# Half-height matmuls in pairs for the third input block of seven float32 first layers

## The chip, the cores and the metric

The kernel runs on one core of one Trainium2 chip. The metric is the device time of one execution in microseconds; lower is better. A time of the whole is the median of several runs. Times within the kernel come from one profiled execution, whose engines are named PE (TensorE's matmuls), PEld (its weight loads), DVE (VectorE), ACT (ScalarE), POOL (GpSimd) and SP (SyncE).

## The reference, cut to what matters

A gated recurrence with heads of width 40 gives 3072 rows of 320 numbers. Each row is then sent to one of 16 experts, whose network has a first layer of 320 x 1024, a Relu and a second layer of 1024 x 320.

```python
for g in range(G):
    ...
    for e in range(Eg):
        ...
        h = np.maximum(xg[mask_e] @ w1[g, e], 0.0)
        ye = h @ w2[g, e]
        combined = g_w[mask_g][mask_e] * e_w[mask_e]
        tok_idx = np.where(mask_g)[0][mask_e]
        out[tok_idx] = combined[:, None] * ye
```

All of it is float32: N = 3072, D = 320, F = 1024, G = Eg = 4.

## The kernel before, in words

The first third of the kernel is the recurrence in chunks (attention), in 24 units, with the choice of experts running beside it in an order written out by hand. Then `expert` runs for each of the 16 experts, largest first; `CAPS` holds how many rows each may take (the width W). From the third expert on, a scheduler orders the instructions.

An expert's rows are gathered from `x_d` in blocks of up to 128 (`load_x`), transposed on PE and copied to `xhl` (`turn_tasks`, lines 636 to 660), so that the 320 inputs stand on partitions in three blocks of 128, 128 and 64. The third block is stored twice over: `w1` is laid out on the host so that inputs 256 to 319 stand on partitions 0 to 63 and again on 64 to 127, and the rows in `x_d` repeat their last 64 columns in the same way (line 282).

Most experts run the first layer on values split into a high and a low part (float32r), and use the doubled third block for both parts. Experts 9 to 15, named by `FULL`, with W = 160, 144, 144, 144, 128, 128 and 96, run it in plain float32 instead (lines 679 to 688). There the upper half of the third block of `xhl` is set to zero by a GpSimd memset (line 652), and two ACT copies fill the rest (653, 654). For each pair of the eight output blocks, one bank of PSUM takes two halves of W columns, and each half sums three matmuls on all 128 partitions. Then `relu` (lines 670 to 677) reads the bank: ACT writes the Relu as the high part of `hh` (672), DVE subtracts to get the low part (675), in one or two instructions. After each pair one piece of the split of the next expert's `w2` is issued (`between`: an ACT cast at 611 and a DVE subtraction at 613). When the first layer has been issued, the next expert's transposes follow (`then`), and after them the second layer (lines 740 to 748), the scaling of `y` (752 to 756) and the scatter into the output (551).

PSUM has eight banks. `ps_1` holds two (`lg`, `av`) throughout. While attention runs, six more hold its scores, `Cp` and `avT`. `close_attention` gives those six to `ps_t` (one, for transposes, tile `tp`), `ps_h` (three, tile `psh`) and `ps_o` (two, tile `po`). The order in which the pools are opened decides which of the old banks each one gets.

Two lines of attention serve as comparison below: `scores` (line 182) multiplies float32 tiles of 40 rows that lie on partitions 0 to 39 and 64 to 103 in turn, into two banks; `values` (line 231) and `state` (line 204) use all rows and 40 or 41 columns; the filling matmuls `busy` (line 130) use the whole array in bfloat16.

Of the kernel before, what the change touches and what calls it, by code (L numbers as in the profile page):

```python
# [7 lines left out]
F32 = mybir.dt.float32  # L8
# [7 lines left out]
PSUM = bass.MemoryType.PSUM  # L16
DRAM = bass.MemoryType.DRAM

P = 128
# [6 lines left out]
F = 1024  # L26
# [27 lines left out]
FULL = (9, 10, 11, 12, 13, 14, 15)  # L54
# [7 lines left out]
def lstm_moe(ctx: ExitStack, tc: tile.TileContext, gates, qkT, nat, wcat, w1, w2, cst, seq, out):  # L62
    nc = tc.nc
    enter = ctx.enter_context
    mm = nc.tensor.matmul
# [32 lines left out]
    ps_1 = enter(tc.tile_pool(name="ps_1", bufs=1, space=PSUM))  # L98
# [24 lines left out]
    pools = {}  # L123
# [140 lines left out]
    def turned(tp, x, cols=(0, P, 2 * P)):  # L264
        for k, o in enumerate(cols):
            ins = nc.tensor.transpose(out=tp[:, k, :], in_=x[:, o:o + P], identity=ident)  # L266
        return ins
# [18 lines left out]
    chores, backs = [], []  # L286

    def bank_of(tag):
        return (pools["t"] if tag == "tp" else ps_1).tile([P, 512], F32, name=tag)

    def logits(u, o, bank):
        for k in range(3):
# [343 lines left out]
    def turn_tasks(key, W, xg, banks=None):  # L636
        t = {}

        def one(i, o, m):
            if i == 0:  # L640
                pool = pools["xhl"][len(xhls) % len(pools["xhl"])]
                sh, dt = ([P, 3, W], F32) if key[0] in FULL else ([P, 3, 2, W], F32R)
                t["x"] = xhls[key] = pool.tile(sh, dt, name="xhl", bufs=1)
            xhl, g = t["x"], xg[i]
            if banks:
                tp = banks[i][:, 0:3 * P].rearrange("p (k t) -> p k t", k=3)
            else:
                tp = bank_of(("tp", "lg", "av")[i])[:, 0:3 * P].rearrange("p (k t) -> p k t", k=3)
            turned(tp, g)
            if key[0] in FULL:  # L650
                if i == 0:
                    nc.gpsimd.memset(xhl[64:P, 2, :], 0.0)
                nc.scalar.copy(xhl[:, 0:2, o:o + m], tp[:, 0:2, 0:m])
                nc.scalar.copy(xhl[0:64, 2, o:o + m], tp[0:64, 2, 0:m])
                return
            xh = xhl[:, :, 0, o:o + m]
            nc.scalar.copy(xh, tp[:, :, 0:m])
            nc.vector.tensor_tensor(xhl[:, :, 1, o:o + m], tp[:, :, 0:m], xh.bitcast(F32), op=ALU.subtract)

        return [lambda i=i, o=o, m=m: one(i, o, m) for i, (o, m) in enumerate(blocks(W))]  # L660

    def expert(key, W, ws, xg, idx, between=(), then=None, last=None):
        xhl = xhls[key]
# [6 lines left out]
        def relu(f, per, src):  # L670
            hr = hh[:, f:f + per, 0:W]
            act = nc.scalar.activation(hr, src, AF.Relu)  # L672
            for dst, t in ((slice(W + mp, 2 * W), slice(0, nf)), (slice(W, W + mp), slice(nf, W))):
                if t.start < t.stop:
                    nc.vector.scalar_tensor_tensor(hh[:, f:f + per, dst], src[:, :, t], 0.0, hr.bitcast(F32)[:, :, t],  # L675
                                                   op0=ALU.max, op1=ALU.subtract)
            return act

        if key[0] in FULL:
            w1s = w1st[key[0]]  # L680
            for f in range(0, NF, 2):
                ps = pools["ps_h"].tile([P, 512], F32, name="psh")
                for g in range(2):
                    for k in range(3):
                        s = slice(k * F + (f + g) * P, k * F + (f + g + 1) * P)
                        ins = mm(ps[:, g * W:(g + 1) * W], w1s[:, s], xhl[:, k, :], start=(k == 0), stop=(k == 2))  # L686
                relu(f, 2, ps[:, 0:2 * W].rearrange("p (q w) -> p q w", q=2))
                do(between, 1)
        elif key in NARROW:
            xw, xh = [xhl[:, k].rearrange("p a w -> p (a w)") for k in range(3)], [xhl[:, k, 0, :] for k in range(2)]  # L690
            for f in range(0, NF, 2):
                hs = pools["hp"].tile([P, 2, W], F32, name="hs", bufs=2)
                for g in range(2):
                    ps = pools["ps_h"].tile([P, 512], F32, name="psh")
                    s0 = slice((f + g) * P, (f + g + 1) * P)
                    s1 = slice(F + (f + g) * P, F + (f + g + 1) * P)
                    mm(ps[:, 0:2 * W], w1h[:, s0], xw[0], start=True, stop=False)
                    mm(ps[:, 0:W], w1l[:, s0], xh[0], start=False, stop=False)
                    mm(ps[:, 0:W], w1l[:, s1], xh[1], start=False, stop=False)
                    mm(ps[:, 0:2 * W], w1h[:, s1], xw[1], start=False, stop=False)  # L700
                    ins = mm(ps[:, 0:2 * W], wsk[:, s0], xw[2], start=False, stop=True)
                    nc.scalar.copy(hs[:, g, :], ps[:, W:2 * W])
                    nc.vector.tensor_tensor(hs[:, g, :], hs[:, g, :], ps[:, 0:W], op=ALU.add)
                act = relu(f, 2, hs)
                if key[0] == 0:
                    do(between, 1)
        else:
            per = 2 if W <= 256 else 1
            for f in range(0, NF, per):
                ps = pools["ps_h"].tile([P, 512], F32, name="psh")  # L710
                for g in range(per):
                    s0 = slice((f + g) * P, (f + g + 1) * P)
                    s1 = slice(F + (f + g) * P, F + (f + g + 1) * P)
                    xh, xl = [xhl[:, k, 0, :] for k in range(3)], [xhl[:, k, 1, :] for k in range(3)]
                    todo = [(w1h, s0, xh[0]), (w1h, s0, xl[0]), (w1h, s1, xh[1]), (w1h, s1, xl[1]), (wsk, s0, xh[2]),
                            (wsk, s0, xl[2]), (w1l, s0, xh[0]), (w1l, s1, xh[1])]
                    for n, (w, s, x) in enumerate(todo):
                        ins = mm(ps[:, g * W:(g + 1) * W], w[:, s], x, start=(n == 0), stop=(n == len(todo) - 1))  # L718
                relu(f, per, ps[:, 0:per * W].rearrange("p (q w) -> p q w", q=per))
                if per == 2 or f % 2:  # L720
                    do(between, 1)
# [8 lines left out]
        for i, (o, m) in enumerate(blocks(W)):  # L730
            t = slice(o, o + m)
            tl = slice(W + mp + o, W + mp + o + m)
            po = pools["ps_o"].tile([P, DM], F32, name="po")
            for f in range(NF):
                s = slice(f * DM, (f + 1) * DM)
# [3 lines left out]
                if m > 64:  # L739
                    mm(po[0:m], hh[:, f, t], w2h[:, s], start=st0, stop=False)  # L740
                    mm(po[0:m], hh[:, f, t], w2l[:, s], start=False, stop=False)  # L741
                    ins = mm(po[0:m], hh[:, f, tl], w2h[:, s], start=False, stop=sp0)  # L742
# [202 lines left out]
    pools["ws"] = [wsa]  # L945
    pools["xhl"] = [mxp]

    def close_attention():
        att.close()
        pools["t"] = enter(tc.tile_pool(name="ps_t", bufs=1, space=PSUM, reuse_waits="tile"))  # L950
        pools["hp"] = enter(tc.tile_pool(name="hp", bufs=1, reuse_waits="tile"))
        pools["ws"].append(enter(tc.tile_pool(name="wsb", bufs=1, reuse_waits="tile")))
        pools["xhl"].append(pools["hp"])
        pools["ps_h"] = enter(tc.tile_pool(name="ps_h", bufs=3, space=PSUM, reuse_waits="tile"))
        pools["ps_o"] = enter(tc.tile_pool(name="ps_o", bufs=2, space=PSUM, reuse_waits="tile"))

    late_ix = {}

# [87 lines left out]
        expert((1, 0), CAPS[1], wsp_[1], xgs[1], ix_of(1), rest, turn_tasks((2, 0), CAPS[2], xgs[2]), done)  # L1046
    rt["manual"] = False
    for r in range(NEARLY + 1, NE):
        if r + 2 < NE:
            load_e(r + 2)  # L1050
            load_ix(r + 2)
            if r not in FULL:
                load_w1(r + 2)
            load_w2(r + 2)
            xgs[r + 2] = load_x(CAPS[r + 2], ix_of(r + 2))
        if r + 1 < NE:
            split = split_tasks(r + 1)
            if r + 1 not in FULL:
                do(split, 3)
            then = turn_tasks((r + 1, 0), CAPS[r + 1], xgs[r + 1])  # L1060
        else:
            then = []
        if r in FULL and r + 2 < NE:
            then.append(lambda r=r: load_w1(r + 2))
        expert((r, 0), CAPS[r], wsp_[r], xgs[r], ix_of(r), split, then)
# [7 lines left out]
    def plain(w1s, w2s, xT):  # L1073
        h = hp.tile([P, NF, P], F32, name="hh")
        for f in range(NF):
            ps = pools["ps_h"].tile([P, 512], F32, name="psh")
            for k in range(3):
                kk = min(P, DM - k * P)
                mm(ps[:, 0:P], w1s[0:kk, k * F + f * P:k * F + (f + 1) * P], xT[0:kk, k, :], start=(k == 0),
                   stop=(k == 2))  # L1080
            nc.vector.tensor_scalar(h[:, f, :], ps[:, 0:P], 0.0, None, op0=ALU.max)
        po = pools["ps_o"].tile([P, DM], F32, name="po")
        for f in range(NF):
            mm(po, h[:, f, :], w2s[:, f * DM:(f + 1) * DM], start=(f == 0), stop=(f == NF - 1))
        return po
# [202 lines left out]
```

## Time and profile before

| | us |
|---|---|
| median of 3 runs (370.94 to 371.11) | 370.95 |
| profiled execution | 368.52 |
| its span, first to last instruction | 366.9 |
| PE busy | 351.4 |
| DVE busy | 247.9 |
| ACT busy | 185.7 |
| POOL busy | 140.7 |

A group of instructions is read as: source line, engine, operation, output<-inputs, shape of the output and input (partitions x elements; for matmuls rows*columns of the stationary operand, then partitions x elements of the moving one), and xcount. Busy time counts overlapping instructions once. Matmuls are pipelined: the next one starts before the last one's end, so the pace is read from starts. The trace shows each float32 matmul as two, with a weight load before each.

### The profile page before, as it was taken

The page shows a single profiled execution, that of the slowest core. Times are in us where ns is not written, and L with a number is a line of the kernel's source. Part 1 is how long each engine was busy: PE and PEld are TensorE (multiplying, and loading weights), DVE is VectorE, ACT ScalarE, POOL GpSimd, SP SyncE. Part 2 cuts the span into 40 slices and gives each one's busy share as a digit, 9 for nine tenths or more (in the row PEclk, how much of TensorE's full clock was granted, in tenths as well). Part 3 has the DMA queues.
Part 4 walks back from the last instruction along what each step waited for, and adds up shares of the span by engine and source line. Part 5 has one row for each costly group of instructions (what it writes and reads, how often), then busy time and mean ns, then how long its engine had stood idle before and what let it go on. Part 6 is the DMA issues. An engine that isn't in the chain of part 4 may idle for free.

```text
span 366.9 us, 9390 instructions
## 1 busy us (share of the span) xinstructions
PE 351.4 (96%) x3572; PEld 318.5 (87%) x3572; DVE 247.9 (68%) x641; ACT 185.7 (51%) x447; POOL 140.7 (38%) x196
## 2 busy tenths in 40 slices
PE   7988999999997999999999999999999999999993
PEld 3766777777775999999999999999999999999992
DVE  6777977999898688577967566765646553365410
ACT  2534445365454363558557466755747454255520
POOL 2354355554664065732234445051223252224111
PEclk9999999999999899999999999999999999999999
DMA  6886787499694705990499765775552678667500
GB/s 191 268 267 248 221 263 274 138 324 301 169 319 127 329 3 195 321 346 31 155 413 397 260 237 208 261 260 171 205 172 66 238 290 326 244 211 289 191 19 17
DMA packets 26407, 82.23 MB, mean 224 GB/s; under 512 B 8528, under 2 KB 12131, under 8 KB 22514
## 3 DMA queue, kind: packets, MB, share of 16 engines
q1 hardware_dynamic: 17794, 60.32, 47.7%
q0 software_dynamic: 4848, 16.05, 12.4%
q10 hardware_dynamic: 3712, 5.18, 4.1%
q8 instruction: 30, 0.49, 0.5%
q14 instruction: 23, 0.19, 0.1%
HBM read 72.70 MB, written 9.10 MB: 223 GB/s over the span
## 4 chain that ended last, share of the span: by engine, by line
PE 62%; DMA 13%; issue 10%; DVE 8%; POOL 3%; ACT 1%; POOLq 1%; SPq 0%; DVEq 0%; ACTq 0%
PE psh L718 11%; PE psh L686 8%; DMA xg<-x_d,ix 6%; PE po L741 6%; PE po L742 6%; PE po L740 6%; PE sp L182 4%; DMA itab<-ent,slot 3%; PE avT L231 3%; PE po L746 2%; PE av L239 2%; DMA x_d<-x 2%; PE av L266 2%; PE po L745 2%; PE Cp L204 1%
## 5 line engine op out<-in xcount | busy, mean ns | idle before, releaser
L551 POOL DMA_INDIRECT out_dram<-y,ix x32 | 38.3, 1196 | 73.9 <-ACT y L752 58.5
L740 PE MATMUL po<-w2h,hh 128*128 128x320 f32 (+3 forms) x200 | 63.0, 315 | 0.0
L742 PE MATMUL po<-w2h,hh 128*128 128x320 f32 (+3 forms) x200 | 61.9, 309 | 0.0
L741 PE MATMUL po<-w2l,hh 128*128 128x320 f32 (+3 forms) x200 | 61.8, 309 | 0.0
L547 POOL DMA_INDIRECT xg<-x_d,ix x32 | 35.2, 1100 | 66.0 <-DMA ix<-itab 30.7
L613 DVE TENSOR_TENSOR w2l<-w2s,w2h 128x640 fp32r<-128x640 f32 x64 | 50.2, 815 | 10.9 <-ACT w2h L611 10.8
L675 DVE SCALAR_TENSOR_TENSOR hh<-psh,hh 128x240 fp32r<-128x240 f32 (+6 forms) x108 | 36.3, 365 | 22.4 <-ACT hh L672 19.7
L672 ACT ACTIVATE hh<-psh 128x288 fp32r<-128x288 f32 (+8 forms) x68 | 30.2, 444 | 34.0 <-PE psh L718 14.6
L611 ACT CAST w2h<-w2s 128x640 fp32r<-128x640 f32 x64 | 43.1, 722 | 0.0
L686 PE MATMUL psh<-xhl,w1s 128*128 128x144 f32 (+3 forms) x336 | 41.3, 283 | 0.0
L686 PEld LDWEIGHTS psh<-xhl,w1s 128*128 128x128 f32 x336 | 40.9, 191 | 0.0
L718 PE MATMUL psh<-xhl,w1h 128*128 128x256 f32 (+5 forms) x224 | 37.8, 291 | 0.4 <-DVE ewi L520 0.4
L740 PEld LDWEIGHTS po<-w2h,hh 128*128 128x128 f32 (+3 forms) x200 | 36.0, 180 | 0.0
L742 PEld LDWEIGHTS po<-w2h,hh 128*128 128x128 f32 (+3 forms) x200 | 35.9, 180 | 0.1
L741 PEld LDWEIGHTS po<-w2l,hh 128*128 128x128 f32 (+3 forms) x200 | 36.0, 180 | 0.0
L752 ACT ACTIVATE y<-po,ix 128x320 f32<-128x320 f32 (+3 forms) x24 | 12.7, 528 | 44.2 <-PE po L742 36.5
L187 DVE TENSOR_TENSOR pt<-sp,cs 128x512 f32<-128x512 f32 x48 | 30.6, 678 | 3.3 <-PE sp L182 3.3
L718 PEld LDWEIGHTS psh<-xhl,w1h 128*128 128x128 f32 x224 | 31.8, 193 | 0.9 <-PE psh L718 0.7
L452 POOL DMA_INDIRECT itab<-ent,slot x24 | 25.3, 1052 | 18.2 <-DVE ohs L375 10.4
L182 PE MATMUL sp<-qk 40*128 40x128 f32 x384 | 28.4, 285 | 0.2
L182 PEld LDWEIGHTS sp<-qk 40*128 40x128 f32 x384 | 23.6, 187 | 4.7 <-issue 3.3
L755 DVE TENSOR_TENSOR y<-y,po 32x320 f32<-32x320 f32 (+1 forms) x8 | 3.8, 475 | 33.9 <-ACT y L754 30.4
(215 smaller groups left out, 711.1 us busy)
## 6 DMA issues: line engine op xcount, KB each, us to landing
w1s<-in_w_dram SPq DMA_DIRECT2D x13, 1536.0 KB
w2s<-in_w_dram SPq DMA_DIRECT2D x13, 1280.0 KB
nt<-in_nat_dram SPq DMA_DIRECT2D x24, 480.0 KB
qk<-in_qkT_dram SPq DMA_DIRECT2D x48, 160.0 KB
x_d<-x ACTq DMA_DIRECT2D x12, 384.0 KB
w1s<-in_w_dram POOLq DMA_DIRECT2D x2, 1536.0 KB
w2s<-in_w_dram POOLq DMA_DIRECT2D x2, 1280.0 KB
w1s<-in_w_dram SPq DMA_DIRECT2D x4, 384.0 KB
```

Of the source, the lines that this page charges most:

```text
L182: mm(t["pm"][r][:, pr, :], qk[rs, 0, pr, :], qk[rs, 1, pr, :], start=True, stop=True)
L187: nc.vector.tensor_tensor(pt, t["pm"][r], bc(cs[:, C_UP:C_UP + P].unsqueeze(1), (P, 4, P)), op=ALU.mult)
L547: return nc.gpsimd.indirect_dma_start(out=o, out_offset=None, in_=src, in_offset=bass.IndirectOffsetOnAxis(ap=idx, axis=0))
L551: return nc.gpsimd.indirect_dma_start(out=out, out_offset=bass.IndirectOffsetOnAxis(ap=idx, axis=0), in_=y, in_offset=None, bounds_check=N ...
L611: nc.scalar.copy(a, src[:, s])
L613: lows.append(lambda: nc.vector.tensor_tensor(o[rows], src[rows, s], a[rows].bitcast(F32), op=ALU.subtract))
L675: nc.vector.scalar_tensor_tensor(hh[:, f:f + per, dst], src[:, :, t], 0.0, hr.bitcast(F32)[:, :, t], op0=ALU.max, op1=ALU.subtract)
L686: ins = mm(ps[:, g * W:(g + 1) * W], w1s[:, s], xhl[:, k, :], start=(k == 0), stop=(k == 2))
L718: ins = mm(ps[:, g * W:(g + 1) * W], w[:, s], x, start=(n == 0), stop=(n == len(todo) - 1))
L740: mm(po[0:m], hh[:, f, t], w2h[:, s], start=st0, stop=False)
L741: mm(po[0:m], hh[:, f, t], w2l[:, s], start=False, stop=False)
L742: ins = mm(po[0:m], hh[:, f, tl], w2h[:, s], start=False, stop=sp0)
```

## The change

In the first layers of experts 9 to 15 the third input block is multiplied on 64 partitions: for the even output block on partitions 0 to 63, for the odd one on 64 to 127. The two output blocks of a pair get a PSUM bank each, so a buffer is two banks. The order within a pair becomes: blocks 0 and 1 of the even one, blocks 0 and 1 of the odd one, then the two half-height matmuls one after the other. The upper half of the third block is now used, so the memset goes, and one copy moves all three parts. The pools `ps_t` and `ps_h` are closed before expert 9, and a new pool of two buffers of two banks takes their four; from there on transposes use the banks of `lg` and `av`. So that this is possible `ps_o` is opened first. `plain`, which no row reaches with these inputs, takes its bank from the new pool.

```diff
     def bank_of(tag):
-        return (pools["t"] if tag == "tp" else ps_1).tile([P, 512], F32, name=tag)
+        if tag == "tp" and "t" in pools:
+            return pools["t"].tile([P, 512], F32, name=tag)
+        return ps_1.tile([P, 512], F32, name="lg" if tag == "tp" else tag)
...
-                tp = bank_of(("tp", "lg", "av")[i])[:, 0:3 * P].rearrange("p (k t) -> p k t", k=3)
+                tp = bank_of(("tp", "lg", "av")[i if "t" in pools else i + 1])[:, 0:3 * P].rearrange("p (k t) -> p k t", k=3)
             turned(tp, g)
             if key[0] in FULL:
-                if i == 0:
-                    nc.gpsimd.memset(xhl[64:P, 2, :], 0.0)
-                nc.scalar.copy(xhl[:, 0:2, o:o + m], tp[:, 0:2, 0:m])
-                nc.scalar.copy(xhl[0:64, 2, o:o + m], tp[0:64, 2, 0:m])
+                nc.scalar.copy(xhl[:, :, o:o + m], tp[:, :, 0:m])
                 return
...
             for f in range(0, NF, 2):
-                ps = pools["ps_h"].tile([P, 512], F32, name="psh")
-                for g in range(2):
-                    for k in range(3):
-                        s = slice(k * F + (f + g) * P, k * F + (f + g + 1) * P)
-                        ins = mm(ps[:, g * W:(g + 1) * W], w1s[:, s], xhl[:, k, :], start=(k == 0), stop=(k == 2))
-                relu(f, 2, ps[:, 0:2 * W].rearrange("p (q w) -> p q w", q=2))
+                ps = pools["ps_h"].tile([P, 2, 512], F32, name="psf")
+                for k, g in ((0, 0), (1, 0), (0, 1), (1, 1), (2, 0), (2, 1)):
+                    s = slice(k * F + (f + g) * P, k * F + (f + g + 1) * P)
+                    rs = slice(0, P) if k < 2 else slice(64 * g, 64 * g + 64)
+                    ins = mm(ps[:, g, 0:W], w1s[rs, s], xhl[rs, k, :], start=(k == 0), stop=(k == 2))
+                relu(f, 2, ps[:, :, 0:W])
                 do(between, 1)
...
+    narrow = ExitStack()
+
     def close_attention():
         att.close()
-        pools["t"] = enter(tc.tile_pool(name="ps_t", bufs=1, space=PSUM, reuse_waits="tile"))
+        pools["ps_o"] = enter(tc.tile_pool(name="ps_o", bufs=2, space=PSUM, reuse_waits="tile"))
+        pools["t"] = narrow.enter_context(tc.tile_pool(name="ps_t", bufs=1, space=PSUM, reuse_waits="tile"))
         pools["hp"] = enter(tc.tile_pool(name="hp", bufs=1, reuse_waits="tile"))
         pools["ws"].append(enter(tc.tile_pool(name="wsb", bufs=1, reuse_waits="tile")))
         pools["xhl"].append(pools["hp"])
-        pools["ps_h"] = enter(tc.tile_pool(name="ps_h", bufs=3, space=PSUM, reuse_waits="tile"))
-        pools["ps_o"] = enter(tc.tile_pool(name="ps_o", bufs=2, space=PSUM, reuse_waits="tile"))
+        pools["ps_h"] = narrow.enter_context(tc.tile_pool(name="ps_h", bufs=3, space=PSUM, reuse_waits="tile"))
...
     for r in range(NEARLY + 1, NE):
+        if r == FULL[0]:
+            narrow.close()
+            del pools["t"]
+            pools["ps_h"] = enter(tc.tile_pool(name="ps_f", bufs=2, space=PSUM, reuse_waits="tile"))
```

## Rows read from the trace of the kernel before

**Rows 1.** The page, part 1: busy us (share of the span) x instructions.

```profile
PE 351.4 (96%) x3572; PEld 318.5 (87%) x3572; DVE 247.9 (68%) x641; ACT 185.7 (51%) x447; POOL 140.7 (38%) x196
```

**Rows 2.** Table by stage: stretch, length, PE, PEld, DVE, ACT, POOL, clock, DMA, GB/s.

```profile
0.00:118.00 118.00, 111.19 (x1773) 83.88 (x1773) 98.60 (x302) 54.00 (x174) 58.90 (x113) 1.00 0.75 238
...
283.25:356.90 73.65, 73.65 (x574) 72.09 (x573) 33.79 (x77) 33.58 (x80) 19.21 (x21) 1.00 0.62 227
```

**Rows 3.** Chain of waits, from 280 us: start, length, what.

```profile
283.41 6.52 PE psh L686 x48
...
361.41 0.85 POOL out_dram L551
```

**Rows 4.** Table by stretch of line 686 alone: length, PE, PEld, clock, DMA, GB/s.

```profile
283.25:289.77 6.52, 6.52 (x48) 6.44 (x48) 1.00 0.61 225
308.67:314.55 5.88, 5.88 (x48) 5.82 (x48) 1.00 0.62 231
333.09:338.44 5.35, 5.35 (x48) 5.32 (x48) 1.00 0.75 273
351.50:356.80 5.30, 5.30 (x48) 5.30 (x48) 1.00 0.08 30
```

**Rows 5.** Timeline of PE: start, length, line, operation; expert 9's and 14's first layers.

```profile
283.11 0.31 PE L746 MATMUL po<-w2h,hh 128*128 128x320 f32 x1
283.25 6.68 PE L686 MATMUL psh<-xhl,w1s 128*128 128x160 f32 x48
...
342.29 5.52 PE L686 MATMUL psh<-xhl,w1s 128*128 128x128 f32 x48
```

**Rows 6.** Timeline of one unit's scores and the two matmuls before them.

```profile
47.62 0.28 PE L231 MATMUL avT<-pt,vz 128*41 128x128 f32 x2
47.83 0.97 PEld L182 LDWEIGHTS sp<-qk 40*128 40x128 f32 x16 [0.19 <-issue]
47.83 1.16 PE L182 MATMUL sp<-qk 40*128 40x128 f32 x16
```

**Rows 7.** Instructions of line 182: duration in ns, shortest/median/longest, first and last start.

```profile
L182 PE MATMUL sp<-qk x384: 272/272/373, 7.0 to 113.0; 40*128 40x128 f32 x192
```

**Rows 8.** Timeline: from scores to matmuls on all rows, twice.

```profile
7.89 0.28 PE L182 MATMUL sp<-qk 40*128 40x128 f32 x2
8.10 0.10 PEld L130 LDWEIGHTS <-ones_b 128*128 128x128 bf16 x1
...
85.16 0.61 PE L182 MATMUL sp<-qk 40*128 40x128 f32 x8
...
85.70 0.14 PEld L266 LDWEIGHTS av<-cs,x 128*128 128x128 f32 x1
85.71 0.33 PE L266 MATMUL av<-cs,x 128*128 128x128 f32 x1
```

**Rows 9.** Timeline: from matmuls of 41 columns to a transpose.

```profile
45.75 0.20 PE L204 MATMUL Cp<-vz,nt 128*40 128x41 f32 x1
45.88 0.42 PEld L239 LDWEIGHTS av<-cs,avs 128*128 128x128 f32 x4
```

**Rows 10.** Timeline of DVE: low parts, second pair of expert 11, first of expert 14.

```profile
312.95 0.51 DVE L675 SCALAR_TENSOR_TENSOR hh<-psh,hh 128x224 fp32r<-128x224 f32 x2
...
345.14 0.42 DVE L675 SCALAR_TENSOR_TENSOR hh<-psh,hh 128x256 fp32r<-128x256 f32 x1
```

**Rows 11.** Instructions of line 652: duration in ns, shortest/median/longest, first and last start.

```profile
L652 POOL MEMSET xhl<- x7: 172/212/253, 263.1 to 338.7; 64x144 f32 x3, 64x128 f32 x2, 64x160 f32 x1, 64x96 f32 x1
```

**Rows 12.** Groups by line and shape, ACT, 283.25 to 357: busy us, mean ns, idle.

```profile
L654 ACT COPY xhl<-tp 64x112 f32<-64x112 f32 x3 | 0.7, 245 | 0.0
```

**Rows 13.** Timeline where attention closes.

```profile
120.25 1.09 DVE L658 TENSOR_TENSOR xhl<-Cp,xhl 128x384 fp32r<-128x384 f32 x2 [1.66 <-ACT xhl L657]
120.88 0.85 PE L266 MATMUL tp<-cs,x 128*128 128x128 f32 x3
121.38 1.20 PE L718 MATMUL psh<-xhl,w1h 128*128 128x256 f32 x4
```

More of the change, by code (lines that the diff above doesn't have):

```diff
@@ L1075, in plain @@
         for f in range(NF):
-            ps = pools["ps_h"].tile([P, 512], F32, name="psh")
+            ps = pools["ps_h"].tile([P, 2, 512], F32, name="psf")[:, 0]
             for k in range(3):
```

## The prediction, made before the change was run

> **What bounds the kernel now.** First the page: TensorE is busy 96% of the span [rows 1]. That share is a mean, so next the table by stage [rows 2]: from 283.25 to 356.90, the stage of experts 9 to 15 that the change rewrites, PE is busy for 73.65 of 73.65 us at granted clock 1.00, its 2.4 GHz level. DVE and ACT are busy less than half of it, and the DMA share is 0.62. Nothing ends a wait there, because PE does not wait. The chain of waits says the same: each first layer (L686) stands in it as one unbroken piece, that of expert 9 as 6.52 us, and the chain ends with the last scatter [rows 3]. So a microsecond more or less of PE in this stage is one more or less at the end. All the L686 time, by its four widths, is 6.52 + 3 x 5.88 + 2 x 5.35 + 5.30 = 40.2 us [rows 4].
>
> **How PE spends it.** Each expert has 8 output blocks x 3 input blocks = 24 matmuls in the source and 48 in the trace [rows 4]: a float32 matmul runs as two, each with a weight load of its own. Start to start they take p = 6.52/48 = 0.136 us at 160 columns, 0.1225 at 144, 0.1115 at 128 and 0.1105 at 96. The loads lie under the matmul before. A group's border costs nothing here: from L746 to L686 it is 0.14 us [rows 5].
>
> **Part 1: the third input block on row halves.** Per pair of output blocks the old order has 6 source matmuls, 12 starts at p. The new has 8 on all rows, then the third block's two source matmuls (4 starts) with 64 rows each, on different halves and into different banks. Do two such run beside each other? The score matmuls (L182) are the same form: float32, 128 weight columns, row halves taken in turn, two banks. Sixteen of them take 1.16 us from first start to last end, with single ones of 0.272 [rows 6, 7]: (1.16 - 0.27)/8 = 0.11 per pair, and two start within 0.01 us (the last two take 0.28 together, [rows 8]). So four starts become two. Saved: 2p per pair of blocks, four pairs per expert: 4 x 2 x (0.136 + 3 x 0.1225 + 2 x 0.1115 + 0.1105) = **6.7 us**, a sixth of 40.2.
>
> Next, what a change from all rows to half rows and back costs, since there is one in each direction per pair of blocks: 4 x 2 x 7 = 56. The attention stage has such changes. The last two L231 start at 47.62, and the first weight load of L182 starts at 47.83: 0.20 later, where inside a group it comes at once. Then that first matmul lasts 0.37 instead of 0.27 (272 ns median, 373 longest), because its load no longer lies under anything: 0.10 more [rows 6, 7]. Back from half rows to all rows: L182 ends at 85.77, so its last started at 85.50, and the load of L266 starts at 85.70: again 0.20 [rows 8]. Is that a wait for data? L182 to L130 at 8.10 needs nothing of the scores, and shows 7.89 to 8.10, 0.21 with the pair's own 0.01 [rows 8]. Where the last matmul is 41 columns wide the gap is 0.13 (45.75 to 45.88, [rows 9]); so it is 0.093 after the last stream's end, at 0.84 ns a column. It is a drain, and it comes with the change of shape of the array's use, not with the group: the border of [rows 5] has none.
>
> The Trainium skill, TensorEngine Tiling (Array Packing), Key Properties, says that changing the tiling mode, unlike changing the tile, drains TensorE. The trace agrees, with 0.20 us at 128 columns. TensorE: Matmul & The Clock Gate of the Trainium skill, step-by-step part, puts the drain at some 128 cycles, which is 0.053 us at 2.4 GHz (an estimate from that page) against 0.093 here; by it the sum below would be 56 x 0.04 = 2.2 us lower, and the rows decide.
>
> One change thus costs c = drain + 0.10 - p. At 128 columns: 0.20 + 0.10 - 0.11 = 0.19. At 144 the drain is 0.213 and p 0.1225: 0.19. At 160: 0.227 and 0.136: 0.19. At 96: 0.173 and 0.11: 0.16. The pair's offset adds 0.007. Net for a pair of blocks, 2c + 0.007 - 2p: +0.166 at 128, +0.148 at 144, +0.121 at 160, +0.113 at 96. Four pairs, seven experts: 4 x (0.121 + 3 x 0.148 + 2 x 0.166 + 0.113) = **+4.0 us**. The last change back of experts 9 to 14 meets the transposes, whose load shows 0.33 instead of 0.27, so 0.05 and not 0.10 [rows 8]: -0.3. Part 1: **+3.7**.
>
> **Part 2: banks.** Two buffers of two banks replace three of one, so a pair of blocks waits for the Relu and the subtraction of the pair before last, no longer of the third last. Queued behind that wait is all of PE. In expert 14 (PE from 342.29 [rows 5], 12 x 0.1115 = 1.34 per pair) DVE reads the first pair until 345.14 + 0.42 = 345.56 [rows 10]. The third pair started at 344.97, 0.59 too early for two buffers. With the longer pairs of part 1 (1.50) it starts at 345.30, 0.26 short. In a 144-wide expert (PE from 308.67) the second pair is read until 312.95 + 0.51 = 313.46 [rows 10] and the fourth would start at 308.67 + 3 x 1.618 = 313.52, just free. DVE and ACT are late because the w2 split stands ahead of them, and that queue empties the sooner the slower PE goes. Bounds: 0, and 0.59 in each of six experts, 3.5. I take **+0.3**, near the expert-14 row alone.
>
> **Part 3: no clearing, one copy.** Seven GpSimd memsets of 0.17 to 0.25 us go; PE waits for nothing in this stage [rows 2], so not for them, and behind them on that queue only scatters wait, which need a later `y` anyway [rows 11]. The two copies per gathered block become one over three parts; on ACT that saves some 0.2 us each for eleven blocks [rows 12], after the first layer, with 3.8 us or more before its result is read (expert 13's L686 ends at 338.44, expert 14's starts at 342.29, [rows 4, 5]). 0. If that cover went, 0.2 per expert. The transposes now take the `lg` and `av` banks, which nothing else uses then: 0.
>
> **Part 4: pools in another order.** When attention closes, the `tp` and `psh` tiles take banks that other tiles held, the `Cp` pair among them. `Cp` is read by DVE from 120.25 to 121.34; the transposes into `tp` start at 120.88 and the first `psh` matmul at 121.38 [rows 13]. The first reading is over before 120.9, the second before 121.38. Bounds 0 to 0.5 (`tp` behind both readings); I take 0.
>
> **The sum.** 3.7 + 0.3 = +4.0 us. The profiled execution took 368.52 us (span 366.9) and would take 372.5. The median of the runs shown, 370.95, lies 2.4 above it; added to that: **375.0 us**, 1.1% slower.
>
> **Rivals.** (a) *Two buffers bite.* The wait of part 2 in most experts at its upper bound: up to 378.2. For it: 0.59 at expert 14 [rows 10]. Against: PE itself becomes slower. 8%. (b) *The halves run one after the other*, or overlap by half, since each source matmul is two: 3.4 to 6.7 of the saving lost, 378.3 to 381.7. Against: [rows 7], eight pairs in eight slots. 3%. (c) *Faster: the next weights load during the drain.* A change then costs 0.09, not 0.19: 56 x 0.10 = 5.6 less, 369.4. It decides at 6.7/56 = 0.12 us per change: below it the change wins. For it: inside a group the load does run ahead. Against: in every change of shape shown the load starts behind the drain, with nothing to wait for in [rows 8]. 6%. (d) *Changes of shape cost nothing in a dense stream*: -6.7, 364.3. The same rows speak against it. 3%. The Trainium skill's same tiling page, Theoretical Speedup, names up to 2x for a small dimension of 64 or less, which is this case's result if nothing is paid around the pair. (e) *The drain is shorter than in attention*, some 0.04 each: 372.8, still slower. 4%. (f) The array stays in one shape and the halves run as before: pairs cost what they cost, within 0.2% of 370.95. 2%.
>
> **Chances and range.** The forecast itself has 74%. A measurement of this kernel tells about 0.2% (0.74 us) from no change. Slower: 74 + 8 + 3 + 4 = 89%; same 2% and a little from (c)'s upper end, 3%; faster 8%. The forecast's own spread is 373.9 to 376.5 (part 2 from 0 to 1, part 4, 0.01 us per change). For 8 in 10 it reaches a little into (e) and (a): 373.4 to 377.3.
>
> **What would show it.** After, an L686-like group at 144 columns takes 5.88 + 4 x 0.148 = 6.5 us instead of 5.88, at 128 some 6.0; the 64-row matmuls come in twos 0.01 us apart; 0.20 us of PEld idle stands before each first 64-row load and 0.2 before each return; the other stages are unchanged; the granted clock stays at 1.00, as it does in the first 118 us with all their changes of shape [rows 2]. Wrong: 64-row loads that start while full-row matmuls still stream (c, d), twos 0.11 apart (b), or PE waiting for DVE in the third or fourth pair by more than 0.3 (a).

## The result, and the profile after

The changed kernel takes 374.6 us (median of 4 runs) beside 370.94 for the kernel before: a ratio of 1.013, 95% interval 1.009 to 1.017. Slower, as forecast, and 0.4 us from the 375.0 on record. In a later set of runs, beside the second half of the experiments below, the medians were 376.85 and 370.11, the ratio 1.016, interval 1.008 to 1.024. Medians here and below are over all runs, while ratios, intervals and spreads leave out slow runs, which lie over 1.5% above the fastest of their kernel (two of the six behind 376.85; the other four have a median of 375.44).

The profiled execution took 373.16 us, span 371.5, against 368.52 and 366.9. Page, part 1, of the changed kernel (busy us, share of the span, instructions), to set beside [rows 1]:

```profile
PE 357.1 (96%) x3572; PEld 315.7 (85%) x3572; DVE 249.2 (67%) x641; ACT 185.6 (50%) x436; POOL 138.7 (37%) x189
```

The share of PE is the same and says nothing; its time is 5.7 us longer with the same number of instructions, while PEld's is shorter. Even the 5.7 is not the price of the change: 1.9 of it lie in the first 118 us (113.08 here, 111.19 in [rows 2]), where nothing was changed. The table by stage, with the columns of [rows 2], shows the stage that was rewritten:

```profile
0.00:118.00 118.00, 113.08 (x1772) 84.85 (x1772) 98.56 (x297) 54.06 (x174) 58.53 (x111) 0.99 0.77 236
283.71:364.90 81.19, 81.18 (x597) 71.70 (x595) 34.32 (x78) 33.75 (x72) 19.25 (x16) 1.00 0.56 206
```

(The second stretch also takes in the last second layer, which the one in [rows 2] does not.) PE is still taken for all of it, at granted clock 1.00, and PEld now stands still for 9.5 us of it. A time that hardly depends on what came earlier in the run is the length of this stage, from the first L686 (L685 after) to the start of the last matmul of the second layer. Timeline of PE, last matmul, of the kernel before and then of the changed one:

```profile
360.20 0.31 PE L742 MATMUL po<-w2h,hh 128*96 128x320 f32 x1
```

```profile
364.59 0.30 PE L741 MATMUL po<-w2h,hh 128*96 128x320 f32 x1
```

Before: 360.20 - 283.25 = 76.95 us ([rows 5] has the start). After: 364.59 - 283.71 = 80.88 us, and 80.88 again in the second profile of the changed kernel (285.35 to 366.23). The change costs **3.93 us** there. The rest of the difference of the two spans, 0.7 us, lies outside: 0.46 before the stage begins and 0.2 behind its last matmul.

Inside a pair of blocks, in expert 10 (144 columns), the timeline shows how the 3.93 comes about. PE, taken in short windows, then PEld. Rows of short windows overlap: the first holds the last matmul on all rows and the two half-height ones behind it; in the others x2 is one pair:

```profile
298.06 0.61 PE L685 MATMUL psf<-xhl,w1s 128*128 128x144 f32 x3
298.27 0.39 PE L685 MATMUL psf<-xhl,w1s 64*128 64x144 f32 x2
298.50 0.29 PE L685 MATMUL psf<-xhl,w1s 64*128 64x144 f32 x2
298.72 0.39 PE L685 MATMUL psf<-xhl,w1s 128*128 128x144 f32 x1
```

```profile
298.27 0.19 PEld L685 LDWEIGHTS psf<-xhl,w1s 64*128 64x128 f32 x2
298.38 0.19 PEld L685 LDWEIGHTS psf<-xhl,w1s 64*128 64x128 f32 x2
298.72 0.19 PEld L685 LDWEIGHTS psf<-xhl,w1s 128*128 128x128 f32 x1
```

The last matmul on all rows starts at 298.06 and the first load for half rows at 298.27: 0.21 later, where the working had 0.213 for this width. The next load follows at 298.38, so the first one held its matmul up by 0.1; that matmul lasts 0.39 and the second 0.29. Both halves of a pair start within 0.01 us (two take 0.39 and 0.29 together). From the second pair at 298.50 to the next load on all rows it is 0.22, the drain again with the pair's own offset. The second and the third pair of blocks of this expert take 1.62 us from first start to first start, where 12 x 0.1225 = 1.47 stood (the first pair takes 1.52, since its first load still lies under the matmul before).

One thing in the PE timeline of this expert was not foreseen:

```profile
297.20 4.83 PE L685 MATMUL psf<-xhl,w1s 128*128 128x144 f32 x36
301.96 0.40 PE L739 MATMUL po<-w2h,hh 128*112 128x320 f32 x1
302.36 1.59 PE L685 MATMUL psf<-xhl,w1s 128*128 128x144 f32 x12
```

Between the third and the fourth pair of blocks the scheduler has put the first matmuls of the second layer, which were ready, into the place where it reckoned with a wait for a buffer. No such wait is in the trace. In the table of waits of this stage (who, for whom: us in total, times, longest; short gaps are left out) the row of the first layer's loads names no reader of a bank, only gaps in which nothing is waited for:

```profile
PEld psf L685 <- issue: 1.0, 6, 0.2
```

### The profile page after: what moved, and what is told of

The parts are those of the page before. It is cut to its first block, busy times and chain, and to the rows that moved or that the text cites. A ratio compares the mean times of both kernels' runs of the same rounds, so it can differ in the third digit from the quotient of the medians.

```text
span 371.5 us, 9357 instructions
## 1 busy us (share of the span) xinstructions
PE 357.1 (96%) x3572; PEld 315.7 (85%) x3572; DVE 249.2 (67%) x641; ACT 185.6 (50%) x436; POOL 138.7 (37%) x189
## 4 chain that ended last, share of the span: by engine, by line
PE 69%; issue 12%; DVE 7%; DMA 5%; POOL 4%; ACT 1%; POOLq 1%; SPq 0%; DVEq 0%
PE psh L717 14%; PE po L739 7%; PE psf L685 7%; PE po L740 7%; PE po L741 7%; PE sp L182 3%; PE avT L231 3%; PE po L745 2%; PE av L266 2%; PE av L239 2%; PE po L744 2%; DMA itab<-ent,slot 2%; PE busy L130 2%; PE avT L222 2%; DMA ix<-itab 2%
## 5 line engine op out<-in xcount | busy, mean ns | idle before, releaser
L553 POOL DMA_INDIRECT out_dram<-y,ix x32 | 37.1, 1161 | 90.4 <-ACT y L751 74.8
L685 PE MATMUL psf<-xhl,w1s 128*128 128x144 f32 (+3 forms) x336 | 44.1, 303 | 0.0
L685 PEld LDWEIGHTS psf<-xhl,w1s 128*128 128x128 f32 x336 | 37.3, 188 | 5.9 <-issue 1.0
L674 DVE SCALAR_TENSOR_TENSOR hh<-psh,hh 128x240 fp32r<-128x240 f32 (+4 forms) x64 | 23.0, 390 | 9.8 <-ACT hh L671 9.7
L671 ACT ACTIVATE hh<-psh 128x512 fp32r<-128x512 f32 (+5 forms) x40 | 19.1, 479 | 17.3 <-PE psh L717 14.7
L231 PE MATMUL avT<-pt,vz 128*41 128x128 f32 x384 | 26.9, 281 | 0.9 <-DVE pt L187 0.7
```

The lines of the kernel that those rows point to most:

```text
L231: mm(placed(pr, r), t["vz"][:, head(pr, r), :], t["pm"][r][:, pr, :], start=(c == 0 and pr < 2), stop=True, skip_group_check=True)
L553: return nc.gpsimd.indirect_dma_start(out=out, out_offset=bass.IndirectOffsetOnAxis(ap=idx, axis=0), in_=y, in_offset=None, bounds_check=N ...
L685: ins = mm(ps[:, g, 0:W], w1s[rs, s], xhl[rs, k, :], start=(k == 0), stop=(k == 2))
```

## The experiments

All kernels below are timed against the kernel before on the same chip; its median was 371.64 beside the first four and 370.11 beside the others, where the table has the 370.94 of the first runs. For each, the stage is measured as above, in one profile, and lengths are taken before rounding. Some expectations name 73.5 us for this stage before (and 75.4, 77.5 or 69.3 after): they count it to about the end of the last first layer, some 3.4 us earlier, so their differences compare with those here and their lengths do not. Whole times of one kernel spread by several us from run to run (366.87 to 372.34 for the kernel before in the second set), and in the profiles the stage begins anywhere between 283.25 and 288.30, so the stage is what is read first.

| kernel | first and last start of the stage | stage, us | against before | median, us | ratio to before (95%) |
|---|---|---|---|---|---|
| before | 283.25, 360.20 | 76.95 | | 370.94 | |
| changed | 283.71, 364.59 | 80.88 | +3.93 | 374.6 | 1.013 (1.009 to 1.017) |
| all rows, two buffers | 287.33, 366.22 | 78.88 | +1.93 | 373.27 | 1.007 (1.003 to 1.011) |
| both on the same half | 284.44, 371.75 | 87.30 | +10.35 | 381.6 | 1.029 (1.024 to 1.035) |
| halves of two pairs together | 288.30, 367.52 | 79.22 | +2.27 | 376.65 | 1.015 (1.010 to 1.020) |
| all on half rows | 283.37, 367.58 | 84.20 | +7.25 | 378.61 | 1.024 (1.018 to 1.030) |
| all halves first | 284.64, 357.47 | 72.83 | -4.12 | 366.16 | 0.991 (0.987 to 0.996) |
| all rows, four buffers | 284.59, 361.54 | 76.95 | 0.00 | 369.72 | 1.001 (0.997 to 1.005) |
| halves apart | 284.94, 382.95 | 98.00 | +21.05 | 390.2 | 1.057 (1.048 to 1.066) |

The theory: each change between all rows and half rows costs PE some 0.19 us, 56 of them, against 6.7 us saved by the pairs. The rivals: the two buffers, halves that don't run beside each other, and the pools.

### All rows, two buffers

```diff
-                    rs = slice(0, P) if k < 2 else slice(64 * g, 64 * g + 64)
+                    rs = slice(0, P)
```

with the memset and the two copies of the kernel before.

> The changed kernel with the third input block back on all 128 rows (upper half cleared again by the memset, two copies), but the new pools, the two banks per buffer and the new order of matmuls kept. Theory (each change between all rows and half rows costs 0.19 us, 56 of them, against 6.7 us saved): both go, so 370.95 + 0 to 0.5, some 371.2 us, the first layer of a 144-wide expert back at 5.9 us. Rival (two buffers instead of three make PE wait): the loss stays, 374 to 375 us, with PE idle before the third and fourth pair.

Neither came out as stated; the rival was right in kind, but the loss is half of what it named. The stage takes 78.88 us, 1.93 over before, although no shape changes. PE's timeline of expert 10, and the largest entry of PE's loads in the table of waits:

```profile
300.59 4.76 PE L688 MATMUL psf<-xhl,w1s 128*128 128x144 f32 x36
305.10 0.40 PE L742 MATMUL po<-w2h,hh 128*112 128x320 f32 x1
305.55 1.71 PE L688 MATMUL psf<-xhl,w1s 128*128 128x144 f32 x12
```

```profile
PEld psf L688 <- DVE hh L677: 0.6, 2, 0.5
```

The row's 4.76 is 0.2 longer than 35 x 0.1225 and the 0.29 of the last matmul. In each of experts 9 to 14 some 0.3 us goes, to a wait for DVE's reading of the pair before last and to the second-layer matmuls that stand in the gap; most of the single waits are too short for the table. Where they stand can be seen in PE's timeline of the first two pairs and of the start of the third:

```profile
300.59 3.10 PE L688 MATMUL psf<-xhl,w1s 128*128 128x144 f32 x24
303.65 0.48 PE L688 MATMUL psf<-xhl,w1s 128*128 128x144 f32 x2
```

The first two pairs keep the old pace (23 x 0.1225 and the last matmul make 3.10). The third, which takes the first buffer again, could start at 300.59 + 24 x 0.1225 = 303.53; it starts 0.12 late, and its second matmul comes 0.20 behind the first, since a load that had to wait is not hidden. So two buffers do cost something, by themselves, with the faster pairs. The experiment with four buffers, below, takes this up.

### Both halves on the same rows

```diff
-                    rs = slice(0, P) if k < 2 else slice(64 * g, 64 * g + 64)
+                    rs = slice(0, P) if k < 2 else slice(0, 64)
```

> The changed kernel with both half-height matmuls of a pair on partitions 0 to 63, so that they can't run beside each other; the number of changes of shape stays 56. Theory: the saving of 6.7 us goes and the cost stays, 374.6 + 6.7 = 381.3 us. Rival (the two halves ran one after the other in the changed kernel anyway): no difference, 374.6 us.

```profile
298.99 5.55 PE L685 MATMUL psf<-xhl,w1s 128*128 128x144 f32 x36
304.86 1.82 PE L685 MATMUL psf<-xhl,w1s 128*128 128x144 f32 x12
```

The timeline has 5.55 where the changed kernel has 4.83. The stage is 87.30 - 80.88 = 6.42 us longer than the changed kernel's, against 6.7 forecast: the halves do run beside each other, and that is what it is worth. (The pair's offset of 0.007, 28 times, is 0.2 of the difference.)

### Halves of two pairs together

```diff
-                for k, g in ((0, 0), (1, 0), (0, 1), (1, 1), (2, 0), (2, 1)):
+                full, half = ((0, 0), (1, 0), (0, 1), (1, 1)), ((2, 0), (2, 1))
+                todo = half + full if f % 4 else full + half
+                for k, g in todo:
...
```

> The changed kernel with the half-height matmuls of every second pair put ahead of its full-height ones, so that those of two pairs stand together: 28 changes of shape instead of 56, the same matmuls and buffers. Theory: 28 x 0.19 = 5.3 us less, 369.3 us, 0.4% under the kernel before. Rival (the loss comes from the buffers or the banks): no gain, 374 to 375 us, or more, since the fourth pair's buffer is wanted earlier.

The stage is 1.66 us shorter than the changed kernel's, not 5.3. The trace says where the rest went. PE and PEld of expert 10, then DVE:

```profile
304.43 1.48 PEld L687 LDWEIGHTS psf<-xhl,w1s 128*128 128x128 f32 x12 [0.22 <-ACT w2h L613]
306.06 0.40 PE L741 MATMUL po<-w2h,hh 128*112 128x320 f32 x1
306.29 0.31 PE L742 MATMUL po<-w2l,hh 128*112 128x320 f32 x1
306.53 0.30 PEld L687 LDWEIGHTS psf<-xhl,w1s 64*128 64x128 f32 x4 [0.21 <-issue]
```

```profile
303.79 0.52 DVE L674 SCALAR_TENSOR_TENSOR hh<-psf,hh 128x224 fp32r<-128x224 f32 x2
```

The scheduler put its two second-layer matmuls (306.06, 306.29) exactly between the halves that were to stand together, so the shape changes twice more in experts 10 to 13. In experts 9 and 14 its gap lies between the second and the third pair, where no halves meet. That is 36 changes in place of 28: 8 x 0.19 = 1.5 us. And in each of experts 9 to 14 a pair waits for its buffer. In expert 10 it is the third, by some 0.27 us (304.43, idle 0.22, and a load that is not hidden); the row names an ACT cast, but what reads that buffer last is DVE's subtraction, which ends at 304.31. In the six experts these waits are 0.27 to 0.51 us each, some 2.0 in all. Together 3.5, against 3.6 missing. The price of a change stands, but this kernel is no clean test of it.

Its whole time does not show the 1.66 us: 1.015 of the kernel before, like the changed kernel's 1.013. Its stage begins latest of all (288.30), behind a part of the kernel that this experiment does not touch; why is open.

### All on half rows

```diff
-                for k, g in ((0, 0), (1, 0), (0, 1), (1, 1), (2, 0), (2, 1)):
+                for n in range(5):
+                    for r, (k, g) in enumerate((((0, 0), (1, 0), (2, 0), (0, 1), (1, 1))[n], ((0, 0), (1, 0), (0, 1), (1, 1), (2, 1))[n])):
...
+                        rs = slice(64 * r, 64 * r + 64)
+                        ins = mm(ps[:, r, g * W:(g + 1) * W], w1s[rs, s], xhl[rs, k, :], start=(k == 0),
...
+                hs = pools["hp"].tile([P, 2, W], F32, name="hs", bufs=2)
+                nc.scalar.copy(hs, ps[:, 1, 0:2 * W].rearrange("p (q w) -> p q w", q=2))
+                nc.vector.tensor_tensor(hs, hs, ps[:, 0, 0:2 * W].rearrange("p (q w) -> p q w", q=2), op=ALU.add)
+                relu(f, 2, hs)
```

One lower and one upper half are issued side by side, each into a bank of its own, and the two banks are added afterwards.

> The first layers of experts 9 to 15 wholly on half rows: lower halves sum into one bank, upper halves into the other, five slots per pair of output blocks instead of six; ACT copies one bank, DVE adds the other, and Relu and subtraction read the sum. Two changes of shape per expert, 14 in all. Theory: 6.7 us saved, 14 x 0.19 - 0.3 = 2.4 us paid, 366.7 us if the extra copy (0.4) and addition (0.45) per pair lie beside PE. Rival (they do not: at an expert's end the second layer waits for them, some 0.9 us each of seven times, or PE waits for its buffers): 373 us or more.

The rival, and more than it said. Timeline of PE and table of waits:

```profile
297.32 2.72 PE L686 MATMUL psf<-xhl,w1s 64*128 64x144 f32 x40
301.38 3.03 PE L686 MATMUL psf<-xhl,w1s 64*128 64x144 f32 x40 [1.34 <-DVE hs L690]
```

```profile
PEld psf L686 <- DVE hs L690: 10.9, 12, 1.7
PE psf L686 <- DVE hs L690: 8.2, 6, 1.5
```

Two pairs run in 2.72 us, 1.3 a pair, so the array is faster indeed; then PE stands still for 1.34 us until the addition has freed a buffer. In the stage such waits of PE's loads are 10.9 us, in which the array's gain of some 4 us drowns.

### All halves first

```diff
+            pss = [pools["ps_h"].tile([P, 2, 512], F32, name="psf") for _ in range(2)]
...
+            for f in (0, 2, 1, 3, 4, 6, 5, 7):
+                g = f % 4 // 2
+                part(f, 2, slice(64 * g, 64 * g + 64), start=(f % 2 == 0), stop=False)
+            for f in range(NF):
+                for k in range(2):
+                    ins = part(f, k, slice(0, P), start=False, stop=(k == 1))
...
```

A bank holds two output blocks; only the first half-height matmul in a bank starts it afresh.

> The eight half-height matmuls of an expert stand together at its start, four on each half of the rows; a buffer of two banks holds four output blocks, so that no buffer is used twice by one expert. 14 changes of shape instead of 56, no wait for a buffer. Theory: 6.7 us saved, 14 x 0.19 - 0.3 = 2.4 us paid, so 4.3 us under the kernel before, 366.7 us; in the stage of experts 9 to 15 some 69.3 us from the first matmul to the last second layer instead of 73.5. Rival (Relu and subtraction of four blocks at once come too late for the second layer): 1 us per expert given back, 371 to 374 us.

```profile
296.99 5.37 PE L685 MATMUL psf<-xhl,w1s 64*128 64x144 f32 x48
357.47 0.30 PE L750 MATMUL po<-w2h,hh 128*96 128x320 f32 x1
```

As the theory had it: the stage takes 72.83 us, 4.12 less than before (forecast 4.3; 0.09 of the 4.12 comes from the measure, since the drain ahead of the very first half-height load lies before the stage's first start here), the first layer of expert 10 is one piece of 5.37 us where 6.04 stood before, and nothing is put into it. The whole kernel takes 366.16 us beside 370.11, faster than both. The same matmuls as in the changed kernel, in another order, are worth 8.05 us in this stage, 7.96 with that drain counted: 42 changes of shape fewer, at 0.19 each 8.0.

### All rows, four buffers

```diff
-                ps = pools["ps_h"].tile([P, 2, 512], F32, name="psf")
+                ps = pools["ps_h"].tile([P, 512], F32, name="psf")
-                for k, g in ((0, 0), (1, 0), (0, 1), (1, 1), (2, 0), (2, 1)):
+                for k, g in ((0, 0), (1, 0), (2, 0), (0, 1), (1, 1), (2, 1)):
...
-            pools["ps_h"] = enter(tc.tile_pool(name="ps_f", bufs=2, space=PSUM, reuse_waits="tile"))
+            pools["ps_h"] = enter(tc.tile_pool(name="ps_f", bufs=4, space=PSUM, reuse_waits="tile"))
```

Both output blocks of a pair share a bank again, and the order of the matmuls is that of the kernel before; the rest is as in the first experiment.

> All rows for the third input block, as in the kernel before, with the changed order of pools, but four buffers of one bank instead of two of two. Theory (what the all-rows kernel with two buffers lost in this stage, 1.9 us, were waits for buffers): the stage takes 73.5 us as before, 371.0 us in all. Rival (order of matmuls, place of the pools or the transposes' banks cost it): the stage stays at 75.4 us, 372.9 us in all.

```profile
310.01 6.04 PE L688 MATMUL psf<-xhl,w1s 128*128 128x144 f32 x48
```

The stage takes 76.95 us, to the hundredth the kernel before, and the ratio is 1.001. Besides the number of buffers, the order of the matmuls and the one bank per pair went back too, so this run alone does not tell them apart. The timeline of the first experiment does: with the new order and two banks its first two pairs keep the old pace, and what is lost stands ahead of pairs that use a buffer again. So the 1.93 us were the two buffers. And the transposes in the banks of `lg` and `av` cost nothing in this stage.

### Halves apart

```diff
-                for k, g in ((0, 0), (1, 0), (0, 1), (1, 1), (2, 0), (2, 1)):
+                for k, g in ((0, 0), (1, 0), (2, 0), (0, 1), (1, 1), (2, 1)):
```

> The changed kernel with the half-height matmul of each output block right behind that block's own full-height ones, so that no two stand together: 112 changes of shape, none of them shared. Theory: 112 x 0.19 - 0.3 = 21.0 us over the kernel before, 392 us; 10.6 over the kernel with both halves on the same rows. Rival (a change of shape costs nothing by itself, and the pair was slow for another reason): as that kernel, 381 us.

```profile
301.06 6.72 PE L685 MATMUL psf<-xhl,w1s 128*128 128x144 f32 x36
308.11 2.22 PE L685 MATMUL psf<-xhl,w1s 128*128 128x144 f32 x12
```

98.00 us, 21.05 over before (forecast 21.0). Against the kernel with both halves on the same rows, which has the same matmuls and no pairs either, there are 56 changes more and 10.70 us more: **0.191 us for each**. The whole time rests on two runs, 390.2 against 392 expected.

### The changed kernel again

> The changed kernel once more, beside these on one chip: 4.0 us over the kernel before, 375.0 us, its stage of experts 9 to 15 at 77.5 us.

Stage 80.88 us, as in the first profile. In all the ratio of 1.016 puts it 3.0 to 9.0 us over the kernel before, an interval that is wide enough for the 4.0.

## Why the prediction was right, point by point

**The bound.** PE was taken for as good as all of the stage before and after, and what it made there reached the end: the ratios agree, within their intervals, with the differences of the stage, but for the halves of two pairs together, whose whole time is longer than its stage explains. Right, with that one open.

**The saving, 6.7 us.** Shown by the pair on the same rows: 6.42.

**The price of a change of shape, c = 0.19 and 0.16.** Shown three ways: the drain of 0.21 at 144 columns in the trace, the 0.191 of the halves apart, the 8.05 us of all halves first. The attention stage's rows [rows 6, 8, 9] gave it to 0.01 us, though the matmuls there are 40 rows high and other lines. Read from the starts in the changed kernel, a pair between two others costs 0.125 us at 160 columns, 0.154 at 144, 0.172 at 128 and 0.131 at 96 (forecast 0.121, 0.148, 0.166 and 0.113). At 96 two parts of c were off and cancelled in part: the load for half rows comes 0.20 us behind the last start, as at 128 columns, and not 0.173, and a load that is not hidden costs 0.07 there and not 0.10. For 28 pairs the measured nets make 4.25, and 3.95 less the 0.3 for the transposes, which show 0.05 as forecast; the stage's 3.93 is thus part 1 alone, forecast 3.7. (With the terms as the prediction prints them its nets come out 0.002 to 0.007 lower, and their sum 3.9 and not 4.0.) That the next load begins only behind the drain, which rival (c) put in doubt, holds in this dense stream too.

**The buffers, +0.3.** This term was not paid. Alone, with all rows, two buffers cost 1.93 us. In the changed kernel the pairs are 0.15 us longer, the readers are done in time, and nothing is left: the table of waits names no reader of a bank, and the third pair of expert 10 takes no longer than the second. That the sum of 4.0 came within 0.1 of the 3.93 is therefore in part luck: part 1 was 0.2 too low and this term 0.3 too high. The working said that the queue empties sooner the slower PE goes, and that is what happened; but the cost is hidden, not gone. In the halves of two pairs together, where the pairs are shorter again, it came back. So parts 1 and 2 don't add, and a figure for the one holds only beside the other.

**The memset, the copies, the pools and banks, 0.** For the transposes' banks shown by the four buffers, where the stage is the same to 0.01 us. The order of the pools acts earlier, where attention closes, and there the whole time of that kernel (1.001, interval 0.997 to 1.005) is too coarse for the 0.5 us in question. The trace of the changed kernel shows no wait at that place:

```profile
122.63 0.85 PE L266 MATMUL tp<-cs,x 128*128 128x128 f32 x3
123.15 1.22 PE L717 MATMUL psh<-xhl,w1h 128*128 128x256 f32 x4
```

The first `psh` matmul starts 0.52 us behind the transposes, 0.50 before [rows 13]. The memset and the copies were not tried alone; since the pairs make up all of the 3.93, nothing is left for them or for the second-layer matmuls in the gap.

**What missed.** Three of the expectations: the halves of two pairs together (a scheduler fills what it takes for a gap, and there its filling changed the shape twice more in four experts), all on half rows, where the rival came out, and the first experiment, whose loss only four buffers explained. Of the rivals, (b), (c), (d), (e) and (f) fall with the rows of the pair, and (a) falls for this kernel, though the cost it names is real by itself.

The 0.46 us by which the stage began later in the changed profile need not be the change's. In the ten profiles it begins between 283.25 and 288.30, and the nine other than the kernel before, which share the order of pools, differ by as much among themselves. Where attention closes, PE waits for the first gathered rows, and not equally long. Timeline of the kernel before, then of the changed one:

```profile
119.15 1.08 PE L266 MATMUL Cp<-cs,xg 128*128 128x128 f32 x6 [1.12 <-DMA xg<-x_d,ix]
```

```profile
120.57 0.55 PE L266 MATMUL Cp<-cs,xg 128*128 128x128 f32 x3 [2.13 <-DMA xg<-x_d,ix]
```

## What to carry to other kernels

Two half-height float32 matmuls on different row halves do run in the time of one, but TensorE has to run empty on the way into that shape and on the way out, and the first weight load after each is not hidden: 0.19 us each way here, so that a pair that stands alone between full-height matmuls loses 0.15 us where its saving was 0.245. Put all half-height work of a stage together before counting the gain, and see to it that neither the buffers nor the scheduler's filling takes it apart again. Read the price of such a change from any stage of the same kernel that already makes it: the number carried over to 0.01 us. And count the buffers together with the pairs, in one timeline, since either can hide the other.

## What the runs showed of the hardware that was not expected

That two costs on one engine can hide one another so fully: 1.93 us of waits for buffers vanish when each pair of blocks is made 0.15 us slower. And that the length of a stage in which PE never waits comes back to 0.01 us (76.95 twice in different kernels, 80.88 in both profiles of the changed one), while whole times of the kernel before spread by over 5 us.

Not every change of shape costs something. The second layer's matmuls, which stand on all rows, take 32 and 64 weight columns in turn. Timeline of PE in the changed kernel, then PEld:

```profile
296.90 0.31 PE L744 MATMUL po<-w2l,hh 128*32 128x320 f32 x1
297.05 0.31 PE L745 MATMUL po<-w2h,hh 128*64 128x320 f32 x1
```

```profile
296.91 0.14 PEld L745 LDWEIGHTS po<-w2h,hh 128*64 128x64 f32 x1
```

They start 0.15 us apart, and the load for 64 columns lies wholly under the matmul of 32. In attention a change from 40 weight columns to 128 does show the drain [rows 9]. What tells the two apart was not tried.
